# The first sequence of an FFT-mixing and SwiGLU kernel: its unit loop replaced by a written list of steps over eight PSUM banks

## The chip, the cores and the metric

One core of one Trainium2 chip runs one program. The metric is the device time of one execution in microseconds (us). Engine names are those of the profile: PE (TensorE matmul), PEld (TensorE weight load), DVE (VectorE), ACT (ScalarE), POOL (GpSimd), SP (SyncE, which here only issues DMAs).

## The reference

A sequence filter along the time axis, done in frequency space, and a SwiGLU feed-forward layer behind it. Eight sequences of 3008 positions with 256 channels each; the feed-forward layer sees all 24064 positions.

```python
X = np.fft.rfft(x, axis=1)                       # x (8, 3008, 256)
Y = X * (filt_r + 1j * filt_i)[None]
x = np.fft.irfft(Y, n=3008, axis=1).reshape(24064, 256)
xn = x / np.sqrt(np.mean(x * x, -1, keepdims=True) + 1e-06) * rms_g
g = xn @ w_gate                                  # (256, 1536)
out = (g / (1 + np.exp(-g)) * (xn @ w_val)) @ w_out
```

## The kernel before

The transform of length 3008 = 47 x 64 is done as matmuls with tables. Each sequence goes through these units, in this order:

- A: the 64-point step (a0_unit for the first sequence, a_unit for the others), then a change of layout. The first sequence changes layout on the chip: tr0_unit (T), eight groups of PE transposes copied out of PSUM to the tiles t2. The other sequences go through DRAM (z_store, t2_load).
- F: f_unit brings the filter into the layout that the product needs: four PE transposes of 128x128 f32, and two copies to the tile ff. There are twelve: three loads i, filter part f (0 imaginary, 1 real), channel half dh. f_neg (N) makes a negated copy of a piece of ff on POOL, f_last (L) copies one row of it.
- B: b_unit, sixteen units of four matmuls into one PSUM bank: the 47-point step. Unit i is group g = i // 2 of four frequencies and half dh = i % 2.
- P: s_part, two products of the bank with the filter for each unit: e = 0 with the real part, e = 1 with the imaginary part, whose negated copy it also reads. 32 in all. Result in a pair of s tiles.
- Y: yt0_unit, eight matmuls with the identity that add the two products and transpose them, and an eviction to yt.
- I: bi_unit, four matmuls of the inverse 47-point step, and an eviction to uu. After the sixteenth unit, POOL copies a strip of uu to the tile left.

When all of uu is there, t4_first transposes the first four columns on the PE, t4_load transposes all of it by DMA from SP, and first_norm makes the first normalised tile. Then the main loop begins: 8 x 6 x 12 items of the feed-forward layer (gv: gate and value matmuls, Silu on ACT, product on DVE; down: the output matmuls two items later). The mixing work of sequences 1 to 7 is spread over the items of the sequence before by a planner with costs and due times; twelve a_units of sequence 1 fall to the start of the loop, the first two of them before it.

All of it stands in a manual schedule: each engine runs its instructions in the order in which the program issues them. What an instruction waits for comes from its tiles: a tile of a rotating pool of n buffers takes the buffer of the n-th tile before it and waits until that tile's last reader is done, also a reader that stands later in the program.

The POOL queue ahead of the first f_neg is a row of DMA issues: four x_load, six f_load, four loads of tables, then w_load(0) and w_load(1), which load thirds of w_gate and w_val to staging tiles. Staging has four buffers: the three filter tiles, then w_load(0); w_load(1) takes the buffer of filter tile 0. A POOL DMA also waits for the landing of the POOL DMA eight places before it. Behind the loop, w_gain multiplies the staged weights by the norm's gain into wg and wv, two instructions for each third and each of the two weights.

For the first sequence the loop over p (lines 659 to 706) keeps one unit of each kind in flight, with b_unit's bank alternating between two banks:

```python
if 3 <= p < UN:
    b_unit(0, od[p], (0, 3)[p % 2])
    s_part(0, od[p], 1)
...
if 2 <= p < UN + 1:
    yt0_unit(od[p - 2], "A", 1)
...
if 4 <= p < UN + 3:
    bi_unit(0, od[p - 4], "AV"[p == UN + 1], 2)
```

Here "A" is an eviction by ACT, "V" one by DVE. At p == 0 the loop also issues to POOL: the rest of f_neg, w_load(2), wo_load(0) and wo_load(1) (thirds of w_out), x_load(1, 0..2) and the whole of w_gain. After the t4_load transposes, POOL waits for one of them (the copy to seen, line 713) and issues wo_load(2) and x_load(1, 3).

Of the kernel before, what the change touches and what calls it, by code (L numbers as in the profile page):

```python
# [1 line left out]

# [1 line left out]

# [22 lines left out]
K2 = 32  # L27
# [74 lines left out]
def kernel(  # L102
# [31 lines left out]
    xnp = ctx.enter_context(tc.tile_pool(name="xnp", bufs=4))  # L134
    hp = ctx.enter_context(tc.tile_pool(name="hp", bufs=4))
    op = ctx.enter_context(tc.tile_pool(name="op", bufs=2))
    psG = ctx.enter_context(tc.tile_pool(name="psG", bufs=2, space=bass.MemoryType.PSUM))
    psV = ctx.enter_context(tc.tile_pool(name="psV", bufs=2, space=bass.MemoryType.PSUM))
    psO = ctx.enter_context(tc.tile_pool(name="psO", bufs=1, space=bass.MemoryType.PSUM))
    psM = ctx.enter_context(tc.tile_pool(name="psM", bufs=1, space=bass.MemoryType.PSUM))  # L140
    psB = ctx.enter_context(tc.tile_pool(name="psB", bufs=1, space=bass.MemoryType.PSUM))
# [44 lines left out]
            nc.gpsimd.dma_start(t.rearrange("p a d -> p (a d)"), src(N2, XC))  # L186
        st[b]["x"][c] = t

    def bank(i, name):
        pool, tag = ((psM, "mx"), (psG, "pg"), (psV, "pv"), (psB, "mb"), (psO, "po0"))[i]  # L190
        return pool.tile([P, 512], FP32, tag=tag, name=name)

    def copy(eng, out, in_, scale=None):
        if eng == "A":
# [16 lines left out]
        nc.sync.dma_start(dst, st[b]["t1"][c])  # L211

    def t2_tile(b, c):
        if b == 0 and c == 3:
            st[b]["t2"][c] = op.tile([KR, KC, D], FP16, tag="o3", name="t2o")
        else:
            st[b]["t2"][c] = t2p.tile([KR, KC, D], FP16, tag="t2", name="t2")
# [5 lines left out]
    def s_part(b, i, e, eng=None):  # L223
        eng = eng or nc.vector
        g, dh = divmod(i, 2)
        ps, s = st[b]["s"][i]
        fv = ff[:, dh, 4 * g:4 * g + 4, :]
        o = s[e].rearrange("p k (r q) -> p k r q", r=2)
        if e == 0:
            f1 = fv[:, :, 2 * SL:3 * SL].unsqueeze(2).to_broadcast([P, 4, 2, SL])  # L230
            eng.tensor_tensor(out=o, in0=ps, in1=f1, op=ALU.mult)  # L231
        else:
            f2 = fv[:, :, 0:2 * SL].rearrange("p k (r q) -> p k r q", r=2)
            eng.tensor_tensor(out=o, in0=ps[:, :, ::-1, :], in1=f2, op=ALU.mult)  # L234

    def b_unit(b, i, bk=3, e=0):
        g, dh = divmod(i, 2)
        ps = bank(bk, "psb")[:, 0:4 * KR]
        for k in range(4):
            kk = 4 * g + k  # L240
            nc.tensor.matmul(ps[:, ts(k, KR)], st[b]["t2"][kk // KC][:, kk % KC, ds(dh * P, P)],  # L241
                             wb[0:KR, kk, :], start=True, stop=True)
        s = [sp.tile([P, 4, KR], FP16, tag="s%d" % n, name="s%d" % n) for n in range(2)]
        st[b]["s"][i] = (ps.rearrange("p (k r q) -> p k r q", k=4, r=2), s)
        s_part(b, i, e)
# [113 lines left out]
        copy(eng, va[:, dh].rearrange("p k (m i) -> p (k m) i", m=NR)[:, :, 4 * gq:4 * gq + 4],  # L359
             ps.rearrange("p (u t) -> p t u", u=4))  # L360

    def tr0_unit(g, eng):
        pool, tag = ((psO, "po0"), (psO, "po1"), (psM, "mx"))[g % 3]
        ps = pool.tile([KR, 4, 2, P], FP16, tag=tag, name="pst")
        for k in range(4):
            for dh in range(2):
                nc.tensor.transpose(ps[:, k, dh, :], va[:, dh, 4 * g + k, :], ident)  # L367
        c, r = divmod(g, 2)
        if c not in st[0]["t2"]:
            t2_tile(0, c)  # L370
        copy(eng, st[0]["t2"][c][:, 4 * r:4 * r + 4, :].rearrange("p k (e d) -> p k e d", e=2), ps)
# [10 lines left out]
            nc.gpsimd.dma_start(t[:, f].rearrange("p a d -> p (a d)"),  # L382
                                raw(src, row, [[FR4 * D, P], [1, FR4 * D]]))

    def f_unit(i, f, dh, e):
        t = fst[i]
        ps = bank(1 + "AV".index(e), "psf").rearrange("p (a q) -> p a q", a=FR4)
        for a in range(FR4):
            nc.tensor.transpose(ps[:, a, :], t[:, f, a, ds(dh * P, P)], idf)  # L389
        v = ps.rearrange("p a (q s) -> p s a q", s=16)  # L390
        fk = ff[:, dh, 0:K2].rearrange("p (t k) c -> p t k c", k=4)
        fu = ff[:, dh, 1:K2 + 1].rearrange("p (t k) c -> p t k c", k=4)[:, ::-1, ::-1, :]
        lo = SL * (1 + f) + 8 * i
        hi = lo + H
        if i < 2:
            copy(e, fk[:, :, :, lo:lo + 8], v[:, 0:8])
            copy(e, fu[:, :, :, hi:hi + 8], v[:, 8:16])
        else:
            copy(e, fk[:, :, :, lo:lo + 8], v[:, 8:16])
            copy(e, fu[:, :, :, hi:hi + 7], v[:, 0:8, :, 1:8])  # L400
# [6 lines left out]
    def f_neg(k0, n, dhs=(0, 1)):  # L407
        for dh in dhs:
            nc.gpsimd.tensor_scalar(out=ff[:, dh, k0:k0 + n, 0:SL], in0=ff[:, dh, k0:k0 + n, SL:2 * SL],
                                    scalar1=-1.0, scalar2=1.0, op0=ALU.mult, op1=ALU.mult)  # L410
# [122 lines left out]
    def gv(b, m, jt):  # L533
        n = nq(b, m)
        xn = st[b]["xn"][m]
        parts = ((0, 2), (2, 4)) if (b, m, jt) in SPLIT else ((0, n),)
        sg = hp.tile([P, 512], FP16, tag="sg", name="sg")
        hh = hhs[(6 * JT * b + JT * m + jt) % 4]
        made = []
        for q0, q1 in parts:  # L540
            w = (q1 - q0) * P
            pg = psG.tile([P, 512], FP32, tag="pg", name="pg")
            pv = psV.tile([P, 512], FP32, tag="pv", name="pv")
# [53 lines left out]
    def wo_load(q):  # L597
        nc.gpsimd.dma_start(wo[:, ts(q, JT // 3), :],
                            moe_w_out.rearrange("(jt p) d -> p jt d", p=P)[:, ts(q, JT // 3), :])

    def w_gain(q):
        cols = ts(q, DFF // 3)
        t = wst.pop(q)
        for k, dst in enumerate((wg, wv)):
            for dt_ in range(2):
                nc.gpsimd.tensor_scalar(out=dst[:, dt_, cols], in0=t[:, k, dt_, :],
                                        scalar1=gsb[:, dt_:dt_ + 1], scalar2=1.0,
                                        op0=ALU.mult, op1=ALU.mult)

    with tc.manual_schedule():  # L610
        nc.vector.memset(ss3[0], 0.0)
# [44 lines left out]
        a0(3)  # L656
        fill(4)
        a0(4, 5)
        todo = [(i, f, dh) for i in range(2) for f in range(2) for dh in range(2)][:7] + [(2, 0, 0)]
        for u in todo[0:2]:  # L660
            f_unit(*u, "A")
        for g in range(7):
            tr0_unit(g, "V")
            if g < 6:
                f_unit(*todo[g + 2], "A")
        f_neg(4, 4, (0,))
        f_neg(8, 8, (0,))
        UN = K2 // 2
        od = [2, 4, 6, 3, 5, 7, 0, 1] + list(range(8, UN))
        tr0_unit(7, "V")  # L670
        for p in range(2):
            b_unit(0, od[p], (0, 3)[p], 1)
        f_unit(1, 1, 1, "A")
        f_unit(2, 0, 1, "A")
        b_unit(0, od[2], 4, 1)
        f_unit(2, 1, 0, "A")
        for p in range(3):
            s_part(0, od[p], 0)
        for p in range(UN + 3):
            if 3 <= p < UN:  # L680
                b_unit(0, od[p], (0, 3)[p % 2])
                s_part(0, od[p], 1)
            if p == 0:
                f_unit(2, 1, 1, "A")
                f_neg(4, 12, (1,))
                f_last()
                f_neg(0, 4)
                w_load(2)
                wo_load(0)
                f_neg(16, 16)  # L690
                wo_load(1)
                for c in range(3):
                    x_load(1, c)
                for q in range(3):
                    w_gain(q)
            if 2 <= p < UN + 1:
                yt0_unit(od[p - 2], "A", 1)
            if p == UN + 1:
                yt0_unit(UN - 1, "V", 1, slice(0, 2))
                yt0_unit(UN - 1, "A", 0, slice(2, 4))  # L700
            if 4 <= p < UN + 3:
                bi_unit(0, od[p - 4], "AV"[p == UN + 1], 2)
            if UN + 1 <= p < UN + 3:
                fill(1, 1)
# [8 lines left out]
        nc.gpsimd.tensor_copy(out=seen, in_=st[0]["t4"][1][:, 0, 0:4])
        wo_load(2)
        x_load(1, 3)
        first_norm()

        items = [(b, m, jt) for b in range(B) for m in range(6) for jt in range(JT)]
# [166 lines left out]
```

## Time and profile before

| | |
|---|---|
| median of 3 runs | 863.09 us (863.01 to 863.34) |
| the profiled execution's own time | 863.15 us |
| its span, first to last instruction | 861.4 us |
| PE busy in the span | 852.4 us (99%) |
| DVE, ACT, POOL busy | 557.2, 612.4, 297.8 us |
| granted PE clock, mean | 0.999 |
| first F unit on PE | 13.03 us |
| a_unit(1, 0) on PE, behind the last I unit | 38.48 us |
| first gate matmul of the main loop | 43.38 us |

Times inside the span count from its first instruction. The stretch from 13.03 to 43.38 us holds all the work that the diff touches and its tail; from there on the rows follow the planner. A row of the timeline is: start, duration, engine, line, operation, tiles written and read, form, count, and in brackets the engine's idle time before it with what ended it. Start to start of two rows of a busy engine is the price of one instruction there; the duration is a little longer, as the next one starts before the end.

### The profile page before, as it was taken

To read this page: it belongs to the slowest core of one execution; us is meant where nothing else is said; L and a number is where in the kernel's file an instruction comes from. 1 tells how busy PE (TensorE), PEld (TensorE's weight loads), DVE (VectorE), ACT (ScalarE), POOL (GpSimd) and SP (SyncE) were. 2 spreads that over 40 slices of the span, in tenths; PEclk is the share of its full clock that TensorE was granted. 3 is DMA by queue.
4 is the path that set the end of the run, shared out by engine and by line. 5 is a ranking of instruction groups with operands and counts; after the bars stand their busy time and mean duration, and the time that the engine had idled before them with its cause. 6 is when DMAs were issued, how large, how long until landed. Compare 5 with 4: busy or idle time off the path is not lost.

```text
span 861.4 us, 17024 instructions
## 1 busy us (share of the span) xinstructions
PE 852.4 (99%) x6142; PEld 532.2 (62%) x6142; DVE 557.2 (65%) x926; ACT 612.4 (71%) x1339; POOL 297.8 (35%) x346
## 2 busy tenths in 40 slices
PE   8999999999999999999999999999999999999997
PEld 6755666566666666666666666666666666665664
DVE  5857655776666666666666676767666665555554
ACT  4986777787588756887577856888567765777443
POOL 5725742453144322534034430444123430132000
PEclk9999999999999999999999999999999999999999
DMA  9995778765975476656755548433564331521101
GB/s 283 270 204 124 150 164 168 139 130 121 197 137 129 121 150 111 151 107 147 139 127 113 132 98 180 108 87 101 131 127 93 97 70 42 124 54 49 62 25 50
DMA packets 198237, 107.98 MB, mean 125 GB/s; under 512 B 158566, under 2 KB 182520, under 8 KB 198152
## 3 DMA queue, kind: packets, MB, share of 16 engines
q1 hardware_dynamic: 189464, 85.52, 44.1%
q0 software_dynamic: 8544, 21.24, 12.7%
q8 instruction: 48, 0.79, 0.4%
q14 instruction: 37, 0.30, 0.1%
q10 hardware_dynamic: 144, 0.13, 0.0%
HBM read 45.78 MB, written 35.65 MB: 95 GB/s over the span
## 4 chain that ended last, share of the span: by engine, by line
PE 96%; DMA 1%; ACT 1%; DVE 1%; issue 0%; POOL 0%; POOLq 0%
PE po L563 28%; PE pg L546 28%; PE pv L546 28%; PE psb L241 3%; PE psi L285 3%; PE psn L314 2%; PE psa L206 2%; DMA fs<-in_filt_i_dram 1%; PE psy L418 1%; PE psf L389 1%; PE pst L367 0%; ACT sg L550 0%; POOL xc L186 0%; DVE s L231 0%; DVE hh L551 0%
## 5 line engine op out<-in xcount | busy, mean ns | idle before, releaser
L551 DVE TENSOR_TENSOR hh<-pv,sg 128x512 f16<-128x512 f32 (+2 forms) x578 | 391.5, 678 | 286.4 <-ACT sg L550 221.9
L550 ACT ACTIVATE sg<-pg 128x512 f16<-128x512 f32 (+2 forms) x578 | 337.4, 584 | 217.6 <-PE pg L546 213.4
L546 PE MATMUL pg<-xn,wg 128*128 128x512 f16 (+2 forms) x1156 | 338.1, 374 | 0.1
L546 PE MATMUL pv<-xn,wv 128*128 128x512 f16 (+2 forms) x1156 | 338.1, 374 | 0.0
L563 PE MATMUL po<-wo,hh 128*128 128x256 f16 x2256 | 332.7, 273 | 0.0
L563 PEld LDWEIGHTS <-hh 128*128 128x128 f16 x2256 | 213.4, 98 | 105.5 <-issue 0.6
L268 POOL TENSOR_TENSOR ss<-s,s 128x384 f16<-128x384 f16 x112 | 101.9, 911 | 273.2 <-DVE s L234 245.2
L546 PEld LDWEIGHTS <-wv 128*128 128x128 f16 x1156 | 112.9, 98 | 130.7
L546 PEld LDWEIGHTS <-wg 128*128 128x128 f16 x1156 | 111.4, 98 | 17.0 <-issue 0.3
L340 POOL TENSOR_TENSOR xt<-y,rho 128x1024 f16<-128x1024 f32 (+1 forms) x46 | 85.4, 1856 | 2.8
L322 ACT ACTIVATE junk<-y 128x256 f16<-128x256 f32 x180 | 74.3, 413 | 2.8
L231 DVE TENSOR_TENSOR s<-psb,ff 128x384 f16<-128x384 f32 x124 | 67.6, 547 | 0.7 <-ACT ff L195 0.6
L234 DVE TENSOR_TENSOR s<-psb,ff 128x384 f16<-128x384 f32 x124 | 67.6, 546 | 0.0
L195 ACT ACTIVATE uu<-psi 128x384 f16<-128x384 f32 (+1 forms) x127 | 61.6, 486 | 1.5 <-DMA out_dram<-o 0.5
L195 ACT ACTIVATE y<-psn 128x512 f32<-128x512 f32 (+1 forms) x95 | 55.7, 588 | 4.2
L285 PEld LDWEIGHTS <-yt 96*128 96x128 f16 x512 | 35.4, 97 | 26.7 <-issue 1.0
L332 POOL TENSOR_TENSOR rho<-u,mhalf 128x4 f32<-128x4 f32 (+1 forms) x46 | 46.5, 1010 | 3.8
L330 POOL TENSOR_SCALAR u<-ss 128x4 f32<-128x4 f32 (+1 forms) x46 | 8.9, 193 | 104.8 <-ACT junk L322 103.8
L195 ACT ACTIVATE t<-psa 128x512 f16<-128x512 f32 x70 | 41.4, 594 | 3.1 <-PE psa L206 1.7
L285 PE MATMUL psi<-wi,yt 96*128 96x96 f16 x512 | 42.9, 205 | 0.1
L241 PE MATMUL psb<-wb,t 96*128 96x96 f16 x480 | 40.1, 206 | 0.3 <-DVE s L234 0.2
L241 PEld LDWEIGHTS <-t 96*128 96x128 f16 x480 | 28.7, 97 | 12.8 <-DVE s L234 3.3
(101 smaller groups left out, 366.2 us busy)
## 6 DMA issues: line engine op xcount, KB each, us to landing
out_dram<-o SPq DMA_DIRECT2D x40, 512.0 KB, 3.6
xc<-in_x_dram POOLq DMA_DIRECT2D x31, 384.0 KB, 5.6
z_tmp<-t SPq DMA_DIRECT2D x28, 384.0 KB, 2.7
t<-z_tmp SPq DMA_DIRECT2D x28, 384.0 KB, 6.0
out_dram<-o SPq DMA_DIRECT2D x7, 384.0 KB, 2.7
fs<-in_filt_i_dram POOLq DMA_DIRECT2D x3, 512.0 KB, 10.8
fs<-in_filt_r_dram POOLq DMA_DIRECT2D x3, 512.0 KB, 11.2
ws<-in_moe_w_gate_dram POOLq DMA_DIRECT2D x3, 512.0 KB, 9.8
```

Source lines behind the costliest of these rows:

```text
L195: nc.scalar.activation(out=out, in_=in_, func=AXT.Copy, **({} if scale is None else {"scale": scale}))
L231: eng.tensor_tensor(out=o, in0=ps, in1=f1, op=ALU.mult)
L234: eng.tensor_tensor(out=o, in0=ps[:, :, ::-1, :], in1=f2, op=ALU.mult)
L241: nc.tensor.matmul(ps[:, ts(k, KR)], st[b]["t2"][kk // KC][:, kk % KC, ds(dh * P, P)], wb[0:KR, kk, :], start=True, stop=True)
L268: nc.gpsimd.tensor_tensor(out=ss3[g % 3][:, :, dh, 0:KR], in0=s[0], in1=s[1], op=ALU.add)
L285: nc.tensor.matmul(ps[:, k, :], yt[0:KR, k, dh, :], wi[0:KR, 4 * g + k, :], start=True, stop=True)
L322: nc.scalar.activation(out=junk, in_=y[:, i, ts(u, D)], func=AXT.Square, accum_out=ss[:, 2 * i + u:2 * i + u + 1])
L340: nc.gpsimd.tensor_tensor(out=xt[:, 0:n, :], in0=y.rearrange("p a (u d) -> p (a u) d", u=2)[:, 0:n, :], in1=rho[:, 0:n].unsqueeze(2).to_br ...
L546: nc.tensor.matmul(ps[:, 0:w], wt[:, dt_, ts(jt, P)], xn[:, q0:q1, dt_, :], start=(dt_ == 0), stop=(dt_ == 1))
L550: nc.scalar.activation(out=sg[:, c], in_=pg[:, 0:w], func=AXT.Silu)
L551: nc.vector.tensor_tensor(out=hh[:, c], in0=pv[:, 0:w], in1=sg[:, c], op=ALU.mult)
L563: nc.tensor.matmul(po[s4 // 2][:, s4 % 2, :], hh[:, ts(s4, P)], wo[:, jt, :], start=(jt == 0 and s4 % 2 == 0), stop=(jt == JT - 1 and (s4 ...
```

## The change

The loop over p is replaced by a list of 127 steps, walked in order. A step is a letter for the unit, its arguments, its evicting engine (A or V) and, behind a colon, its PSUM bank. The eight banks get names: mx, mb, o0, o1, g0, g1, v0, v1 (the pools psG and psV now have two named tiles of one buffer each, in place of one tile of two buffers; "g" and "v" alone alternate). G is a half of a w_gain third, W, O and X are w_load, wo_load and x_load(1, .), Z is a fill matmul.

Units 8 and 9 carry an "s": b0_unit copies their bank to SBUF by ACT (a tile of the pool xn) and their two products each run on POOL. Two more pairs of s tiles come from the hh tiles of the main loop. Three F units and six T units are evicted by DVE, nine F units and two T units by ACT, and four I units and three halves of Y15 and I15 by DVE. On POOL, f_neg is sixteen instructions of one unit each; wo_load(1), x_load(1, 2), the second half of w_gain(1) and all of w_gain(2) come after the list, and of these wo_load(1), x_load(1, 2) and the last half of w_gain come after the copy to seen.

```diff
-    psG = ctx.enter_context(tc.tile_pool(name="psG", bufs=2, space=bass.MemoryType.PSUM))
-    psV = ctx.enter_context(tc.tile_pool(name="psV", bufs=2, space=bass.MemoryType.PSUM))
+    psG = ctx.enter_context(tc.tile_pool(name="psG", bufs=1, space=bass.MemoryType.PSUM))
+    psV = ctx.enter_context(tc.tile_pool(name="psV", bufs=1, space=bass.MemoryType.PSUM))
...
+    BANKS = {"mx": (psM, "mx"), "mb": (psB, "mb"), "o0": (psO, "po0"), "o1": (psO, "po1"),
+             "g0": (psG, "pg0"), "g1": (psG, "pg1"), "v0": (psV, "pv0"), "v1": (psV, "pv1")}
+    turn = {"g": 0, "v": 0}
...
     def t2_tile(b, c):
-        if b == 0 and c == 3:
+        if b == 0 and len(st[b]["t2"]) == 3:
...
+    def b0_unit(i, bk, soft):
+        g, dh = divmod(i, 2)
+        ps = bank(bk, "psb")[:, 0:4 * KR]
+        for k in range(4):
+            kk = 4 * g + k
+            nc.tensor.matmul(ps[:, ts(k, KR)], st[0]["t2"][kk // KC][:, kk % KC, ds(dh * P, P)],
+                             wb[0:KR, kk, :], start=True, stop=True)
+        if soft:
+            v = xnp.tile([P, 512], FP32, tag="xn", name="v0")[:, 0:4 * KR]
+            copy("A", v, ps)
+            ps = v
+        st[0]["s"][i] = (ps.rearrange("p (k r q) -> p k r q", k=4, r=2), s0_free.pop(0))
...
-    def w_gain(q):
+    def w_gain(q, k):
         cols = ts(q, DFF // 3)
...
-        todo = [(i, f, dh) for i in range(2) for f in range(2) for dh in range(2)][:7] + [(2, 0, 0)]
-        for u in todo[0:2]:
-            f_unit(*u, "A")
-        for g in range(7):
-            tr0_unit(g, "V")
-            if g < 6:
-                f_unit(*todo[g + 2], "A")
...
+        STEPS = """
+            F001A:g0 F000V:g1 T0A:v0 T4V:o1 T6V:v1 T5V:o0 F010A:g1 F100A:v0 T1V:mx T2V:g0 T3V:g1 T7A:v1 F200V:o0
+            F201A:g0 N02 F101V:v0 F110A:v1 B6:mb N03 B4:mx N01 P4.1 F011A:o0 P6.1 B2:o1 P2.1 N11 N06 F210A:v1
+            B3:g1 N16 N13 P3.1 B8s:o0 F111A:g0 F211A:v0 B7:o0 P4.0 N05 N15 P2.0 N04 P6.0 Y4A:mx P7.1 B5:v1 N12
+            Y2A:o1 Y6A:g0 B9s:o1 B10:mx P5.0 P5.1 P8.0 P3.0 L P7.0 N10 P10.1 I4A:mb P8.1 Y5A:v0 I6A:g0 B1:v1
+            Y7A:o1 P10.0 N07 P1.1 W2 Y3A:mb B11:mx N00 B0:g0 I2A:v0 O0 P1.0 P11.0 Y10A:o0 B12:v1 P11.1 P12.1
+            P12.0 I5A:g1 Y8A:mb N17 P0.0 X0 I10A:o0 P0.1 Y1A:v0 P9.0 B13:o1 I3A:mb P13.1 B14:v1 P13.0 Y12A:g1
+            Y11A:mx Y0A:mb P14.1 N14 I7A:o0 P14.0 B15:g0 Y13A:g1 P15.0 P15.1 I12V:v0 X1 G0 G1 G2 Y14A:o1 P9.1
+            I0V:v1 I11V:o0 I8A:mx Y9A:mb I1A:g0 Y15aV:g1 I14A:v0 Y15bV:o1 I13V:mb I9A:v1 I15aV:o0 Z1:mx I15bA:o1"""
+
+        s0_free = [[sp.tile([P, 4, KR], FP16, tag="s%d" % n, name="s%d" % n) for n in range(2)]
+                   for _ in range(4)]
+        s0_free += [[hhs[2 * i + n][:, 0:4 * KR].rearrange("p (k q) -> p k q", k=4) for n in range(2)]
+                    for i in range(2)]
...
+            elif k == "P":
+                u, e = a.split(".")
+                s_part(0, int(u), int(e), nc.gpsimd if u in soft else None)
...
         for c in range(NXC):
             t4_load(0, c)
+        w_gain(1, 1)
+        w_gain(2, 0)
         nc.gpsimd.tensor_copy(out=seen, in_=st[0]["t4"][1][:, 0, 0:4])
+        wo_load(1)
+        x_load(1, 2)
+        x_load(1, 3)
         wo_load(2)
-        x_load(1, 3)
+        w_gain(2, 1)
         first_norm()
```

In the list F201A is filter load 2, part 0, half 1; T4V is group 4; N02 is f_neg of half 0, group 2; P4.1 is unit 4, e = 1; Y15a and Y15b are the two halves of unit 15.

More of the change, by code (lines that the diff above doesn't have):

```diff
@@ L1 @@
 from contextlib import ExitStack
+from functools import partial
 import numpy as np
@@ L187, in x_load, with bank @@
         st[b]["x"][c] = t
-    def bank(i, name):
-        pool, tag = ((psM, "mx"), (psG, "pg"), (psV, "pv"), (psB, "mb"), (psO, "po0"))[i]
-        return pool.tile([P, 512], FP32, tag=tag, name=name)
+    BANKS = {"mx": (psM, "mx"), "mb": (psB, "mb"), "o0": (psO, "po0"), "o1": (psO, "po1"),
+             "g0": (psG, "pg0"), "g1": (psG, "pg1"), "v0": (psV, "pv0"), "v1": (psV, "pv1")}
+    turn = {"g": 0, "v": 0}
+    def bank(i, name, shape=(P, 512), dt=FP32):
+        if not isinstance(i, str):
+            i = ("mx", "g", "v", "mb", "o0")[i]
+        if i in turn:
+            turn[i] += 1
+            i += "01"[turn[i] % 2]
+        pool, tag = BANKS[i]
+        return pool.tile(list(shape), dt, tag=tag, name=name)
     def copy(eng, out, in_, scale=None):
@@ L360, in a0_unit, with tr0_unit @@
              ps.rearrange("p (u t) -> p t u", u=4))
-    def tr0_unit(g, eng):
-        pool, tag = ((psO, "po0"), (psO, "po1"), (psM, "mx"))[g % 3]
-        ps = pool.tile([KR, 4, 2, P], FP16, tag=tag, name="pst")
+    def tr0_unit(g, eng, bk):
+        ps = bank(bk, "pst", (KR, 4, 2, P), FP16)
         for k in range(4):
@@ L383, in f_load, with f_unit @@
                                 raw(src, row, [[FR4 * D, P], [1, FR4 * D]]))
-    def f_unit(i, f, dh, e):
+    def f_unit(i, f, dh, e, bk):
         t = fst[i]
-        ps = bank(1 + "AV".index(e), "psf").rearrange("p (a q) -> p a q", a=FR4)
+        ps = bank(bk, "psf").rearrange("p (a q) -> p a q", a=FR4)
         for a in range(FR4):
@@ L541, in gv @@
             w = (q1 - q0) * P
-            pg = psG.tile([P, 512], FP32, tag="pg", name="pg")
-            pv = psV.tile([P, 512], FP32, tag="pv", name="pv")
+            pg, pv = bank("g", "pg"), bank("v", "pv")
             for ps, wt in ((pg, wg), (pv, wv)):
@@ L599, in wo_load @@
                             moe_w_out.rearrange("(jt p) d -> p jt d", p=P)[:, ts(q, JT // 3), :])
-    def w_gain(q):
+    def w_gain(q, k):
         cols = ts(q, DFF // 3)
[L603 to L608, printed above, removed]
+        for dt_ in range(2):
+            nc.gpsimd.tensor_scalar(out=(wg, wv)[k][:, dt_, cols], in0=wst[q][:, k, dt_, :],
+                                    scalar1=gsb[:, dt_:dt_ + 1], scalar2=1.0, op0=ALU.mult, op1=ALU.mult)
     with tc.manual_schedule():
@@ L658 @@
         a0(4, 5)
-        todo = [(i, f, dh) for i in range(2) for f in range(2) for dh in range(2)][:7] + [(2, 0, 0)]
-        for u in todo[0:2]:
-            f_unit(*u, "A")
-        for g in range(7):
-            tr0_unit(g, "V")
-            if g < 6:
-                f_unit(*todo[g + 2], "A")
[L666 to L685, printed above, removed]
-                f_last()
[L687 to L704, printed above, removed]
@@ L705 @@
-        bi_unit(0, UN - 1, "V", 3, slice(0, 2))
-        bi_unit(0, UN - 1, "A", 0, slice(2, 4))
-        a_unit(1, 0, "A", 1)
+        STEPS = """
[7 more added lines that the diff above has]
+            I0V:v1 I11V:o0 I8A:mx Y9A:mb I1A:g0 Y15aV:g1 I14A:v0 Y15bV:o1 I13V:mb I9A:v1 I15aV:o0 Z1:mx I15bA:o1"""
@@ new lines @@
+        s0_free = [[sp.tile([P, 4, KR], FP16, tag="s%d" % n, name="s%d" % n) for n in range(2)]
+                   for _ in range(4)]
+        s0_free += [[hhs[2 * i + n][:, 0:4 * KR].rearrange("p (k q) -> p k q", k=4) for n in range(2)]
+                    for i in range(2)]
+        halves = {"": slice(0, 4), "a": slice(0, 2), "b": slice(2, 4)}
+        soft = set()
+        for step in STEPS.split():
+            head, _, bk = step.partition(":")
+            k, a = head[0], head[1:]
+            if k == "F":
+                f_unit(int(a[0]), int(a[1]), int(a[2]), a[3], bk)
+            elif k == "T":
+                tr0_unit(int(a[0]), a[1], bk)
+            elif k == "N":
+                f_neg(4 * int(a[1]), 4, (int(a[0]),))
+            elif k == "L":
+                f_last()
+            elif k == "B":
+                if a[-1] == "s":
+                    soft.add(a[:-1])
+                b0_unit(int(a.rstrip("s")), bk, a[-1] == "s")
+            elif k == "P":
+                u, e = a.split(".")
+                s_part(0, int(u), int(e), nc.gpsimd if u in soft else None)
+            elif k == "Y" or k == "I":
+                u = a[:-1].rstrip("ab")
+                (yt0_unit if k == "Y" else partial(bi_unit, 0))(int(u), a[-1], bk, halves[a[len(u):-1]])
+                if k == "Y" and a[len(u):-1] != "a":
+                    s0_free.append(st[0]["s"][int(u)][1])
+            elif k == "Z":
+                fill(int(a), bk)
+            elif k == "W":
+                w_load(int(a))
+            elif k == "O":
+                wo_load(int(a))
+            elif k == "X":
+                x_load(1, int(a))
+            elif k == "G":
+                w_gain(*divmod(int(a), 2))
@@ L708 @@
+        a_unit(1, 0, "A", "g0")
         t4_first()
-        a_unit(1, 1, "V", 0)
-        fill(1, 3)
+        a_unit(1, 1, "V", "mx")
+        fill(1, "mb")
         for c in range(NXC):
             t4_load(0, c)
+        w_gain(1, 1)
+        w_gain(2, 0)
         nc.gpsimd.tensor_copy(out=seen, in_=st[0]["t4"][1][:, 0, 0:4])
+        wo_load(1)
+        x_load(1, 2)
+        x_load(1, 3)
         wo_load(2)
-        x_load(1, 3)
+        w_gain(2, 1)
         first_norm()
```

## The prediction

> **What bounds the kernel now.** First the page, for what the whole program waits for.
>
> ```profile
> PE 852.4 (99%) x6142; PEld 532.2 (62%) x6142; DVE 557.2 (65%) x926; ACT 612.4 (71%) x1339; POOL 297.8 (35%) x346
> ```
>
> The PE is busy for 852.4 of 861.4 us, and from the first gate matmul on it stops for nothing. So the edit can only move the time at which the main loop starts, and add stalls inside the loop. Second, the busy time by stretches (length; PE, PEld, DVE, ACT, POOL busy with counts; PE clock, DMA share, GB/s).
>
> ```profile
> 13.00:21.00 8.00, 7.97 (x108) 7.98 (x109) 5.64 (x9) 5.22 (x17) 4.68 (x8) 1.00 1.04 413
> 21.00:37.00 16.00, 15.03 (x243) 13.22 (x241) 15.31 (x33) 14.59 (x35) 14.12 (x25) 1.00 1.11 316
> 43.40:855.00 811.60, 811.00 (x5651) 500.42 (x5650) 525.15 (x859) 581.18 (x1267) 269.51 (x295) 1.00 0.55 118
> ```
>
> From 21 to 37 us four engines are nearly full at once: PE 15.0, DVE 15.3, ACT 14.6, POOL 14.1 of 16. Work taken from DVE must land where there is room, and POOL has none. Third, the POOL timeline, as POOL is where the change puts it, with the last rows of DVE and two of PE.
>
> ```profile
> 15.35 0.61 PE L389 MATMUL psf<-tab,fs 128*128 128x128 f32 x4
> ...
> 18.59 0.70 POOL L594 DMA_DIRECT2D ws<-in_moe_w_gate_dram  x1 [0.83 <-PE pst L367]
> 19.28 0.72 POOL L594 DMA_DIRECT2D ws<-in_moe_w_val_dram  x1
> 20.28 0.84 POOL L409 TENSOR_SCALAR ff<-ff 128x192 f32<-128x192 f32 x2 [0.27 <-ACT ff L195]
> ...
> 24.04 0.66 POOL L409 TENSOR_SCALAR ff<-ff 128x192 f32<-128x192 f32 x2
> 24.65 0.78 POOL L594 DMA_DIRECT2D ws<-in_moe_w_gate_dram  x1
> 25.43 0.73 POOL L594 DMA_DIRECT2D ws<-in_moe_w_val_dram  x1
> 26.16 0.77 POOL L598 DMA_DIRECT2D wo<-in_moe_w_out_dram  x1
> ...
> 30.95 1.62 POOL L606 TENSOR_SCALAR wg<-ws,gsb 128x512 f16<-128x512 f32 x2
> 32.30 1.57 POOL L606 TENSOR_SCALAR wv<-ws,gsb 128x512 f16<-128x512 f32 x2
> ...
> 36.47 0.54 DVE L234 TENSOR_TENSOR s<-psb,ff 128x384 f16<-128x384 f32 x1
> ...
> 46.02 0.18 POOL L713 COPY seen<-t 128x4 f16<-128x4 f16 x1 [6.64 <-DMA t<-uu]
> ...
> 54.30 0.60 PE L206 MATMUL psa<-xc,tab 128*128 128x512 f16 x2
> ...
> 80.87 1.00 POOL L234 TENSOR_TENSOR s<-y,ff 128x384 f16<-128x384 f32 x1
> ```
>
> w_load(1) (18.59) stands at the head of POOL's queue, and every f_neg and so every e = 1 product is behind it. It waits for two things: the landing of the ninth POOL DMA (issued at 6.30, 11.7 us to landing: 18.0) and the last reader of filter tile 0, which is the fourth F unit of load 0 (at 15.35, so long done). Here the first decides.
>
> **Part 1: the wait of w_load(1).** The list moves that fourth F unit (F011A) behind seven other F units, eight T and two B. In the rows of before a pair of F and T takes 0.89 us on the full PE, so one takes 0.445; a B takes 0.17. F011A is the ninth F: 13.03 + 17 x 0.445 + 0.34 = 20.95, and its end is seen by others 0.17 later (first F pair done on PE 13.03 + 0.45, ACT starts at 13.70): 21.1. The bank of each of these steps is free in time if the evictions take what they take now. A POOL DMA leaves 0.28 us after what it waited for (landing at 6.02, issue at 6.30). So w_load(1) leaves at 21.4, its second half 0.70 later, and N02 starts at 22.9 in place of 20.28: 2.6 us late. Queued behind it on POOL: everything that follows. DVE's first product, P4.1, needs N02, so it starts at 23.3 (21.20 before). DVE has nothing else in its queue meanwhile.
>
> **Part 2: DVE.** Before: 32 products at 0.465 (starts 25.32, 25.79, 26.25), the last ending at 37.0. After: 28 of them = 13.0, so 36.3. Four I units (0.465 each) and three halves (0.3) come on top, 2.8 us, which makes 39.1 with no stall, against 38.96 before. Taking the products of two units off DVE saves 1.9 us and adding evictions gives that back; the late start uses up the rest. F and T on DVE (5.6 us) lie between 13.5 and 20.5, where it idles now.
>
> **Part 3: POOL, which I take to be the new bound.** P9.1, the last soft product, stands behind nearly all of POOL's work, and Y9 on PE needs it. From N02 on, start to start: 16 f_neg pieces at 0.33 = 5.3 (24.04 row); L two copies, 0.4; four products of 128x384 at 0.97 (79.91 to 80.87), 3.9; W2 two DMA issues, 0.78 + 0.73 = 1.5; O0 0.8; X0 and X1 0.55 each, 1.1 (three in 1.65); G0, G1, G2 six instructions at 0.667 (30.95, 32.30, 33.63: two in 1.33) = 4.0. Sum 17.0. The chain has no other wait: the bank copies of units 8 and 9 and the filter tiles are there earlier. P9.1 ends at 22.9 + 17.0 = 39.9. The 16 small pieces of f_neg cost 1.3 us more than the larger pieces of before (768 elements took 0.85, four times 192 take 1.32).
>
> **Part 4: the tail.** Behind Y9 the PE's order has I1, Y15a, I14, Y15b, I13, I9, I15a, Z1, I15b. Y9 to its eviction's start is 0.69 (23.92 to 24.61), then ACT runs Y9 0.49, I1, I14, I9 0.38 each and the half I15b 0.24: 39.95 + 0.69 + 0.49 + 1.14 + 0.24 = 42.5. uu is complete at 39.0 now (ACT's rows end at 39.02). The front is 3.5 us later. t4_first, first_norm and t4_load hang on uu alone, so the first gate matmul goes from 43.38 to 46.9.
>
> **Part 5: loads behind seen.** POOL issues wo_load(1), x_load(1, 2), x_load(1, 3), wo_load(2) behind the copy to seen, in place of wo_load(2), x_load(1, 3). The same transfers, of the same sizes and in the same places, left at 46.15 and 46.94 before, landing 6.0 and 8.2 us later (DMA view: 256 and 384 KB). In times of before, wo_load(1) is there at 52.2 and its first use is the fifth output tile at 53.00: hidden, with 0.8 to spare. x_load(1, 2) is there at 55.1, and a_unit 6 runs at 54.30: the PE, in order, stands still for 0.85. x_load(1, 3) has its use at 57.99 and wo_load(2) at 59.73: hidden, though by one more transfer only. The gain halves are done by 50.3 in the same scale and first used at 56.7.
>
> [...]
>
> **Parts without a row.** T on ACT (128x1024 f16) has no row: at least one 512-wide eviction (0.59) and at most two (1.19); I take 1.0, as 128 elements more cost 0.11 (Y 0.49, I 0.38). Two of them lie beside PE work and no B needs them soon; ACT has 9 F at 0.58, 2 T, 2 copies, 15 Y at 0.49, 11 I at 0.38 and a half I, 19.8 us of work in 28. The two bank copies by ACT are taken as an I (0.38). The eight named banks hold the same memory, and in the main loop g0 and g1 alternate as the two buffers did: nothing. On SP nothing is moved.
>
> **Sum.** Against the profiled execution (863.15, 0.06 above the median): + 3.5 + 0.85 = 867.5. On the low end POOL's pieces at the shortest starts seen (0.31, 0.95) take off 0.4, and no x stall 0.85: 866.2. On the high end pieces under DVE load at 0.5 (the second of the 20.28 pair, with twice the elements) add up to 2: 869.5.
>
> **Rivals.**
>
> *w_load(1) is not held.* For it: its PE wait cost nothing before. Against: the buffer's last reader does move. N02 at 20.28, P9.1 at 37.3, uu at 39.9: + 0.9 + 0.85, 864.9.
>
> *Faster: POOL is not the bound and DVE is.* For it: POOL's spans are rough, and DVE loses 1.9 us. Products from 21.2, 13.0 + 2.8 behind it, uu at 37.0: 2.0 earlier, less the x stall 1.15: 862.0, and 861.1 without it. This needs P9.1 done by 36.4 for break-even and by 34.4 for all of it, so no hold at w_load(1) and POOL's 17.0 at 14.1 or less. Against: POOL's starts are regular, 0.667 six times over.
>
> *The PE clock drops.* Before Y9 the PE has no step left from about 36.6 (Y14 behind P14.0 at 35.5, then I0, I11, I8) until 39.9: an idle gap of 3.3 us, where the longest now is 0.8. The row of before: the last matmul ends at 856.6, the granted clock is 1.00 from 859 to 860 and 0.65 from 860 to 861.4, so a fall to half came about 3.8 us after. A fall would make the tail's matmuls like the first ten fills (4.45 us, 0.22 each when warm): about + 2, 869.5. The decision is whether the gap passes 3.4 to 3.8.
>
> [...]
>
> *x_load(1, 2) lands in time*, as POOL's queue is empty by then: 866.7.
>
> **How the numbers follow.** Forecast 0.54, in time 0.13, clock 0.13, not held 0.08, DVE-bound 0.12. A measurement of this kernel tells 0.2% (1.7 us) from no change. Faster by more takes two thirds of the DVE case, 0.08; half of "not held" and the rest of it fall inside, 0.08; slower 0.84. The range leaves out DVE-bound and the far end of the clock case: 864.4 to 870.5.
>
> **What would show it.** Right: w_load(1) leaves at about 21.4 with a wait for PE, N02 near 22.9, P4.1 near 23.3; POOL has no idle from N02 to P9.1; P9.1 ends near 39.9 and PE's idle ahead of Y9 is 3 us; the first gate matmul is at 46.9; a wait of PE for xc of 0.8 us near a_unit 6. Wrong: P9.1 ends before 37, or DVE's last product of the list rather than POOL's releases the tail, or the loop starts before 43.4.

## The result and the profile after

The changed kernel takes 868.86 us (median of 4 runs, 868.68 to 869.19), the kernel before 863.18 beside it (4 runs, 863.01 to 863.34): a ratio of 1.0066, interval 1.0049 to 1.0084, so it is slower by 0.7%. The profiled execution took 868.68, 5.53 more than the one of before; its span is 866.9. The first gate matmul is at 48.24 (43.38 before), so 4.86 of the 5.53 are there when the main loop starts.

The page's line of engines, for the question whether the PE works more:

```profile
PE 852.4 (98%) x6141; PEld 532.9 (61%) x6141; DVE 558.4 (64%) x930; ACT 611.5 (71%) x1333; POOL 303.2 (35%) x359
```

PE is busy for the same 852.4 us. The 5.5 us that were added are time in which it stands still. The busy time by stretches (PE, PEld, DVE, ACT, POOL with counts, PE clock, DMA share, GB/s) says where:

```profile
13.00:21.00 8.00, 6.89 (x93) 6.77 (x94) 5.99 (x12) 4.52 (x10) 2.54 (x4) 1.00 1.03 411
21.00:37.00 16.00, 13.27 (x201) 12.74 (x200) 12.95 (x29) 11.23 (x29) 14.03 (x30) 0.89 0.76 247
```

From 21 to 37 us POOL alone is as full as before (14.0 of 16); the busy time of PE, DVE and ACT has come down by 1.8, 2.4 and 3.4 us. From 13 to 21 POOL has lost 2.1 us of work: it waits. The timeline of POOL (start, length, line, output and input, count, and in brackets the idle time ahead with what ended it):

```profile
17.31 0.72 POOL L615 DMA_DIRECT2D ws<-in_moe_w_val_dram  x1 [0.54 <-DMA fs<-in_filt_r_dram]
22.70 0.71 POOL L615 DMA_DIRECT2D ws<-in_moe_w_gate_dram  x1 [4.67 <-PE psb L426]
23.40 0.72 POOL L615 DMA_DIRECT2D ws<-in_moe_w_val_dram  x1
24.24 3.50 POOL L418 TENSOR_SCALAR ff<-ff 128x192 f32<-128x192 f32 x11
...
36.20 1.45 POOL L625 TENSOR_SCALAR wg<-ws,gsb 128x512 f16<-128x512 f32 x2
37.55 1.42 POOL L625 TENSOR_SCALAR wv<-ws,gsb 128x512 f16<-128x512 f32 x2
38.88 1.39 POOL L625 TENSOR_SCALAR wg<-ws,gsb 128x512 f16<-128x512 f32 x2
40.20 1.02 POOL L244 TENSOR_TENSOR s<-v,ff 128x384 f16<-128x384 f32 x1
```

w_load(1) stands for 4.67 us at the head of the queue and leaves at 22.70; the first f_neg starts at 24.24, and without a gap from there the last soft product, P9.1, ends at 41.23. The bracket names PE's psb, the B unit that ran last; what the load needs is the filter unit F011A just ahead of it. PE's rows, in order: the four F units from F200 on, F011A, Y4 (the first Y unit), Y9, and a_unit 6 in the loop:

```profile
19.66 1.94 PE L398 MATMUL psf<-tab,fs 128*128 128x128 f32 x16 [0.69 <-DVE t2o L207]
21.77 0.62 PE L398 MATMUL psf<-tab,fs 128*128 128x128 f32 x4
27.11 1.09 PE L440 MATMUL psy<-tab,s 128*96 128x128 f16 x8 [2.57 <-DVE s L241]
41.28 0.59 PE L440 MATMUL psy<-tab,s 128*96 128x128 f16 x7 [1.25 <-POOL s L244]
59.74 0.61 PE L216 MATMUL psa<-xc,tab 128*128 128x512 f16 x2 [0.42 <-DMA xc<-in_x_dram]
```

F011A ends at 22.39, 0.31 ahead of the load's issue. DVE's first product, P4.1, waits for the first f_neg on POOL:

```profile
24.64 1.95 DVE L244 TENSOR_TENSOR s<-psb,ff 128x384 f16<-128x384 f32 x4 [2.69 <-POOL ff L418]
```

Y9 is released by POOL. The chain of waits (start, length, engine, tile, line) ran in the kernel before along PE and, from 35 us, DVE:

```profile
34.63 0.46 PE psy L418 x8
35.09 0.53 DVE s L231
35.62 0.47 DVE s L234
```

In the changed kernel it goes along POOL for 17 us:

```profile
24.24 3.50 POOL ff L418 x11
...
36.26 1.40 POOL wg L625 x2
37.66 1.31 POOL wv L625 x2
38.96 1.31 POOL wg L625 x2
40.27 0.97 POOL s L244
41.28 0.61 PE psy L440 x7
```

Of the part of this chain after 36.26, 4.0 us are w_gain's: work that nobody needs before the loop stands ahead of the product that the loop waits for.

### The profile page after: what moved, and what is told of

It is laid out like the page before. It is cut to its first block, busy times and chain, and to the rows that moved or that the text cites. A ratio compares the mean times of both kernels' runs of the same rounds, so it can differ in the third digit from the quotient of the medians.

```text
span 866.9 us, 17021 instructions
## 1 busy us (share of the span) xinstructions
PE 852.4 (98%) x6141; PEld 532.9 (61%) x6141; DVE 558.4 (64%) x930; ACT 611.5 (71%) x1333; POOL 303.2 (35%) x359
## 3 DMA queue, kind: packets, MB, share of 16 engines
q0 software_dynamic: 8544, 21.24, 12.6%
## 4 chain that ended last, share of the span: by engine, by line
PE 92%; DMA 3%; POOL 2%; ACT 1%; DVE 1%; issue 1%; SPq 0%; POOLq 0%
PE po L584 28%; PE pg L567 27%; PE pv L567 27%; PE psn L324 2%; PE psi L295 2%; PE psb L251 2%; PE psa L216 2%; DMA xc<-in_x_dram 2%; DMA t<-uu 1%; POOL ff L418 1%; PE psf L398 1%; ACT uu L205 0%; POOL xc L187 0%; DVE hh L572 0%; POOL wg L625 0%
## 5 line engine op out<-in xcount | busy, mean ns | idle before, releaser
L244 DVE TENSOR_TENSOR s<-psb,ff 128x384 f16<-128x384 f32 x119 | 64.9, 548 | 2.7 <-POOL ff L418 2.7
L241 DVE TENSOR_TENSOR s<-psb,ff 128x384 f16<-128x384 f32 x119 | 64.9, 547 | 0.3 <-PE psb L426 0.2
L205 ACT ACTIVATE uu<-psi 128x384 f16<-128x384 f32 x124 | 60.2, 488 | 1.1 <-PE psi L295 0.2
L251 PE MATMUL psb<-wb,t 96*128 96x96 f16 x432 | 36.2, 206 | 0.3 <-DVE s L244 0.3
L324 PE MATMUL psn<-t,tab 128*128 128x512 f16 x92 | 34.4, 374 | 0.1
```

The source lines that it names most:

```text
L205: nc.scalar.activation(out=out, in_=in_, func=AXT.Copy, **({} if scale is None else {"scale": scale}))
```

## The experiments

Three things were open: whether the hold of w_load(1) and the order of POOL's queue each carry their share, whether the PE clock had a part in it, and whether the late x_load(1, 2) could be had for nothing. All edits are against the changed kernel, save in e8. "pg0" is the first gate matmul. The kernel before took 863.01, 863.36 and 863.31 in the three groups of runs (e1 to e4; e5 to e8; e9 to e11). Where no interval is given, the time is one run, and the place of pg0 in the trace decides.

**e3, the hold.** F011A goes to right behind F010A, its bank to mb:

```diff
- T5V:o0 F010A:g1 F100A:v0 ... N01 P4.1 F011A:o0 P6.1
+ T5V:o0 F010A:g1 F011A:mb F100A:v0 ... N01 P4.1 P6.1
```

> The changed kernel with the step F011A moved up behind F010A, into bank mb. Theory (w_load(1) holds POOL until the last reader of filter tile 0 is done): w_load(1) leaves at about 20 instead of 22.70, bound by the landing of the ninth POOL DMA; the first f_neg starts at 21.6 instead of 24.24, P9.1 ends 2.6 earlier at 38.6, the first gate matmul at 45.6; no idle of PE over 2 us ahead of Y4 and no drop of its clock. Rival (the landing of the filter loads, 1.5 later than before, sets the start): the first f_neg moves by less than 0.5, the first gate matmul stays near 48.

Measured: 866.82. POOL's timeline:

```profile
18.84 0.70 POOL L615 DMA_DIRECT2D ws<-in_moe_w_gate_dram  x1 [0.82 <-PE pst L376]
20.30 0.72 POOL L615 DMA_DIRECT2D ws<-in_moe_w_val_dram  x1 [0.76 <-DMA wb<-wb_t]
21.14 3.19 POOL L418 TENSOR_SCALAR ff<-ff 128x192 f32<-128x192 f32 x10
...
37.12 1.03 POOL L244 TENSOR_TENSOR s<-v,ff 128x384 f16<-128x384 f32 x1
```

The first f_neg starts 3.10 earlier and P9.1 ends 3.08 earlier, at 38.15: the chain of 17.0 us moves as a whole with w_load(1). The hold is shown (e11, below, has the same edit and ends P9.1 2.77 earlier than the changed kernel). But pg0 came only 1.90 earlier, at 46.34. The windows tell where the rest went:

```profile
35.49:38.90 3.41, 0.95 (x19) 0.81 (x17) 0.80 (x2) 1.16 (x4) 2.66 (x4) 1.00 0.78 145
38.90:42.31 3.41, 3.41 (x34) 2.65 (x32) 1.58 (x4) 2.48 (x6) 0.41 (x2) 0.50 0.03 5
```

The PE now idles 2.46 us ahead of Y9; its clock is halved from 38.90 to 42.31, which is the tail, and the tail (from the end of P9.1 to uu whole) takes 3.69 instead of 2.63.

**e11, the clock in the tail.** e3, with ten filler matmuls, whose result nobody reads, in the gap ahead of Y9:

```diff
- I8A:mx Y9A:mb
+ I8A:mx Z10:mb Y9A:mb
```

> The changed kernel with F011A behind F010A, as in the run before with that edit alone, and ten fill matmuls into the free bank mb ahead of Y9, where PE idled for 2.46 us and its clock then was 0.5 from 38.9 to 42.3. Theory (the tail behind P9.1 took 3.7 us instead of 2.6 because of that clock): P9.1 ends at 38.1 again, the clock stays at 1.00, uu is whole at 40.8 instead of 41.84 and the first gate matmul at 45.2 instead of 46.34. Rival (something else of that order lengthens the tail): the tail stays at 3.7.

Measured: 865.73, and a clock of 1.00 from 8 to 60 us:

```profile
35.20:38.60 3.40, 3.20 (x27) 1.61 (x25) 1.29 (x3) 1.64 (x4) 3.26 (x5) 1.00 0.98 186
```

P9.1 ends 0.31 later than in e3, as the filter load that w_load(1) waits for landed later (19.34, 18.29 in e3); yet pg0 is at 45.48, 0.86 earlier: the tail is back at 2.64. So the clock drop on the tail cost 1.05 us in e3.

**e4, the clock where the changed kernel loses it.** In the changed kernel the clock is halved from 26.63 to 30.04, behind the idle time ahead of Y4. Ten fillers go there:

```diff
- B7:o0 P4.0
+ B7:o0 Z10:v1 P4.0
```

> The changed kernel with ten fill matmuls more, into the free bank v1, behind B7, where PE idles from 24.5 to 27.1 and its granted clock then is 0.5 from 26.6 to 30.0. Theory (POOL's queue): the clock stays at 1.00, DVE's products end about 1 us earlier, at 37.7, and the first gate matmul stays at 48.2 within 0.1, as P9.1 on POOL is where it was. Rival (the clock's drop costs time): the first gate matmul comes 0.7 to 1.4 earlier.

Measured: 870.47. The clock held there and DVE's products ended 1.13 earlier (37.54), but P9.1 ended at 41.05 against 41.23: the cold stretch costs the changed kernel nothing, as POOL sets the end. The time went up since the PE, done with its other work earlier, now idled 2.52 ahead of Y9 and the clock fell on the tail instead (4.0 us; pg0 49.41). The two stretches, before and in the drop:

```profile
37.46:40.87 3.41, 1.13 (x21) 0.93 (x19) 1.61 (x4) 1.97 (x5) 3.41 (x6) 1.00 1.06 200
40.87:44.28 3.41, 3.17 (x34) 3.18 (x35) 1.08 (x3) 1.49 (x4) 0.18 (x1) 0.50 0.10 20
```

**e2, POOL's queue.** w_gain's six instructions go behind P9.1:

```diff
- X1 G0 G1 G2 Y14A:o1 P9.1
+ X1 Y14A:o1 P9.1 G0 G1 G2
```

> The changed kernel with G0, G1, G2 behind P9.1 instead of ahead of it. Theory (POOL's queue releases the tail): P9.1 ends 4.0 us earlier, at 37.2; Y9 then follows I8 on PE at 39.8 instead of 41.28, the first gate matmul comes 1.4 earlier, at 46.8; DVE, whose products end at 38.7, is the next bound, so not all of the 4.0 is seen. Rival (DVE and the cold PE set the front, POOL's wait lies beside them): the first gate matmul stays at 48.2.

Measured: 866.09, pg0 at 45.52. POOL's timeline:

```profile
35.90 1.12 POOL L244 TENSOR_TENSOR s<-v,ff 128x384 f16<-128x384 f32 x1
36.90 1.45 POOL L625 TENSOR_SCALAR wg<-ws,gsb 128x512 f16<-128x512 f32 x2
```

P9.1 ends at 37.02, 4.2 earlier. The loop starts 2.7 earlier, twice what was expected: N02 came 0.3 earlier, and the clock did not drop (1.00 from 8 to 60 us), so that DVE, which is the bound now, ended its products at 37.44 instead of 38.67. A stall of 0.77 ahead of a_unit 6 stayed.

**e6, both.** e3 and e2 together.

> The changed kernel with both: F011A behind F010A, and G0, G1, G2 behind P9.1. Theory: the two terms of POOL's queue are gone, P9.1 ends near 34.2, and DVE's products, which end near 34.7, are the next bound; the tail behind them 3.7, uu whole at 38.4, the first gate matmul at 42.8, 0.6 ahead of the kernel before; the PE's wait for xc at a_unit 6 (0.6 to 0.8) eats that, the span is within 0.4 of the kernel before. Rival (other costs of the list, such as its bank order or ACT's evictions, hold the front): the first gate matmul not before 44.5.

Measured: 863.41, against 863.36 of before. The issue of w_load(1) and P9.1 on POOL:

```profile
19.90 0.70 POOL L615 DMA_DIRECT2D ws<-in_moe_w_gate_dram  x1 [2.14 <-DMA fs<-in_filt_i_dram]
...
33.38 1.11 POOL L244 TENSOR_TENSOR s<-v,ff 128x384 f16<-128x384 f32 x1
```

P9.1 ends at 34.49, DVE's products at 34.97, pg0 is at 43.04, 0.34 ahead of the kernel before; the x stall of 0.59 takes that back. The hold and the order of POOL's queue are together all of what was lost ahead of the loop.

**e5, the soft products back on DVE.**

```diff
- s_part(0, int(u), int(e), nc.gpsimd if u in soft else None)
+ s_part(0, int(u), int(e), None)
```

> The changed kernel with the four soft products of units 8 and 9 on DVE again (the copies of their banks by ACT stay). Theory (POOL's queue releases the tail, and its work is worth less there than the 3.9 us that the four products take): DVE has 32 products from 24.6 on, 14.9 us and 1 us of a cold PE, so its last one ends near 40.5, ahead of POOL's 41.23 in the changed kernel; the first gate matmul at 47.4 to 47.9 instead of 48.24. Rival (DVE is the bound that the soft units relieve): 1.9 us more on DVE, the first gate matmul at 49.5 or later.

Measured: 867.4, pg0 at 47.32. DVE is then the bound: its products end at 40.31, since they start as late as before (N02 24.16). Even so the loop starts 0.9 earlier than with two units on POOL: in this list the two units cost more on POOL, the bound, than they free on DVE.

**e1, the x load.** x_load(1, 2) from behind seen to ahead of w_gain(1, 1):

```diff
+x_load(1, 2)
 w_gain(1, 1)
 w_gain(2, 0)
 nc.gpsimd.tensor_copy(out=seen, in_=st[0]["t4"][1][:, 0, 0:4])
 wo_load(1)
-x_load(1, 2)
 x_load(1, 3)
```

> The changed kernel with x_load(1, 2) moved from behind the copy to seen to right behind the list of steps, ahead of w_gain(1, 1), where POOL is idle. Theory (POOL's queue): the load lands before 50, the wait of PE for xc ahead of a_unit 6 (0.58 us in the changed kernel, 59.16 to 59.74) is gone, the first gate matmul stays at 48.2, the span is 0.6 shorter. Rival (DMA load): the transfer beside the t4_load transposes delays these and the loop's start by as much as it saves, the span stays within 0.2.

Measured: 871.32, 2.6 slower than the changed kernel. The stall ahead of a_unit 6 is gone. But the load leaves at 44.64, beside the t4_load transposes, and their four rows span 11.5 us instead of 8.2, and the copy to seen, which waits for one of them, is at 54.60 instead of 50.89; the rows of SP's queue in the changed kernel and then in e1:

```profile
43.95 8.19 SPq L309 DMA_TRANSPOSE t<-uu  x4
```

```profile
43.80 11.50 SPq L309 DMA_TRANSPOSE t<-uu  x4
```

PE waits for their result, and then for wo_load(1), which POOL issues behind seen, 3.7 later. PE's timeline in e1:

```profile
54.59 0.40 PE L505 MATMUL psn<-tab,t 128*128 128x128 f16 x4 [1.69 <-DMA t<-uu]
...
61.16 0.60 PE L584 MATMUL po<-wo,hh 128*128 128x256 f16 x4 [1.42 <-DMA wo<-in_moe_w_out_dram]
```

The theory that the load could be had for nothing there fell. The rival came true in kind: the transposes were delayed, but the price came inside the loop (pg0 is at 48.09) and was larger than it said.

**e7, three other places at once.** w_load(1) issued behind N12, as its data are needed late; w_gain behind P9.1; all three x loads together, in the place of X0.

```diff
-        w_load(1)
- P7.1 B5:v1 N12 ... N17 P0.0 X0 I10A:o0 ... I12V:v0 X1 G0 G1 G2 Y14A:o1 P9.1
+ P7.1 B5:v1 N12 W1 ... N17 P0.0 X0 X1 X2 I10A:o0 ... I12V:v0 Y14A:o1 P9.1 G0 G1 G2
```

> The changed kernel with w_load(1) issued behind the step N12, so that no f_neg stands behind it; G0, G1, G2 behind P9.1; and x_load(1, 1) and x_load(1, 2) behind x_load(1, 0) in the list, so that x_load(1, 2) is in before the t4_load transposes. Theory: first f_neg at 20 to 21.1, by the landing of the ninth POOL DMA; from there to P9.1 13.0 of the old sum, 1.4 for w_load(1) and 0.55 for the added x_load: P9.1 at 35 to 36.1, uu whole at 37.6 to 38.7, the first gate matmul at 42 to 43.1, no wait of PE for xc at a_unit 6: 0.3 to 1.4 us under the kernel before. Rival (the x loads beside other transfers, or DVE, hold it): first gate matmul after 43.4 or a wait of PE in the loop's first 20 us, not faster than before.

Measured: 863.9 (10 runs, 862.87 to 864.39), ratio to the kernel before 1.0003, interval 0.9993 to 1.0012: no gain, a miss. uu was whole at 38.94, but x_load(1, 0), behind the moved w_load(1) and w_load(2) in the queue and with two more x loads right after it, left at 31.98 and landed at 39.20, and PE's first a_unit of the next sequence waited:

```profile
39.25 0.39 PE L216 MATMUL psa<-xc,tab 128*128 128x512 f16 x1 [0.73 <-DMA xc<-in_x_dram]
```

**e9, the x loads earlier.** e6, with the three x loads ahead of W2 and none behind seen but x_load(1, 3):

```diff
- N07 P1.1 W2 Y3A:mb ... N17 P0.0 X0 I10A:o0
+ N07 P1.1 X0 X1 X2 W2 Y3A:mb ... N17 P0.0 I10A:o0
```

> The changed kernel with F011A behind F010A, G0 to G2 behind P9.1, and x_load(1, 0) to x_load(1, 2) ahead of w_load(2) in the list. Theory: as with the first two alone (first gate matmul 43.04), P9.1 0.5 later by the added x_load and still beside DVE's products, which end near 35; x_load(1, 0) lands near 36, ahead of a_unit(1, 0), and x_load(1, 2) near 41, so neither wait of PE for xc is left: first gate matmul 43.0 to 43.5, the span 0.4 under to 0.2 over the kernel before. Rival (transfers still running at 39 delay t4_load and what hangs on it): a wait of PE in the loop's first 20 us, the span 0.5 or more over.

Measured: 862.87 (10 runs, 862.33 to 863.09), the kernel before 863.31 (19 runs, 863.09 to 863.64); ratio 0.9994, interval 0.9985 to 1.0004. pg0 is at 42.98, 0.40 ahead of before, and no stall follows in the loop. None of its runs is above the lowest of before beside it, but the interval does not exclude 1. It is the best version found, and 6.0 us below the changed kernel. In its POOL timeline the second half of w_load(0) is followed by

```profile
19.83 0.70 POOL L615 DMA_DIRECT2D ws<-in_moe_w_gate_dram  x1 [2.20 <-DMA fs<-in_filt_i_dram]
```

so w_load(1) now waits for the landing of the ninth POOL DMA (the first part of filter load 2, in at 19.27) and no longer for F011A.

**e10, I units on ACT.** e9 with I0 and I11 evicted by ACT, to relieve DVE.

```diff
- I0V:v1 I11V:o0 I8A:mx Y9A:mb
+ I0A:v1 I11A:o0 I8A:mx Y9A:mb
```

> The same with the evictions of I0 and I11 by ACT instead of DVE. Theory (with POOL's terms gone DVE's tail is the bound: 3.7 us behind its last product, 2.8 of it its own evictions): DVE's tail 0.93 shorter, uu whole 0.4 to 0.9 earlier, first gate matmul 42.3 to 42.9, the span 0.4 to 1.0 under the kernel before. Rival (ACT, which gets 0.76 more ahead of Y9, sets the tail): no earlier than without it.

Measured: 863.5 (863.31 to 863.69), ratio 1.0003, interval 0.9994 to 1.0012; pg0 at 43.73. Y9's eviction stands behind three I evictions in ACT's queue, and PE waits for it (0.19 in e9):

```profile
38.07 0.58 PE L295 MATMUL psi<-wi,yt 96*128 96x96 f16 x10 [0.95 <-ACT yt L205]
```

**e8, the hold alone, in the kernel before.** Its list of F units gets the two last readers of filter tiles 0 and 1 exchanged:

```diff
-        todo = [(i, f, dh) for i in range(2) for f in range(2) for dh in range(2)][:7] + [(2, 0, 0)]
+        todo = [(0, 0, 0), (0, 0, 1), (0, 1, 0), (1, 0, 0), (1, 0, 1), (1, 1, 0), (2, 0, 0), (1, 1, 1)]
...
-        f_unit(1, 1, 1, "A")
+        f_unit(0, 1, 1, "A")
```

> The kernel before with the fourth F unit of filter load 0 in the place of the last F unit of load 1, on PE near 20.6 instead of 15.35, and that one in its place. Nothing else is changed. Theory (w_load(1) holds POOL until that unit is done): w_load(1) leaves at 21.4 instead of 18.59, the first f_neg at 22.9 instead of 20.28, DVE's first product near 23.3 instead of 21.20, the first gate matmul 1.0 to 2.0 later than 43.38. Rival (the order of the F units costs nothing by itself, the loss of the change is in its other parts): within 0.3 of 43.38.

Measured: 863.28, pg0 at 43.61, 0.23 later. The expected 1.0 to 2.0 did not come. POOL's row:

```profile
20.04 0.70 POOL L594 DMA_DIRECT2D ws<-in_moe_w_gate_dram  x1 [2.33 <-PE psf L389]
```

The load waited 2.33, though not for F(0,1,1), which is at 20.81 on PE, but for F(1,1,1):

```profile
19.13 0.61 PE L389 MATMUL psf<-tab,fs 128*128 128x128 f32 x4
```

So the load here takes the buffer of tile 1, and not that of tile 0, as the description of the kernel before has it. That fits a load that takes the tile whose last reader stands first in the program; this one run shows it. For the changed kernel, where F011A stands ahead of F111A, both give tile 0. The first f_neg was 1.29 late and DVE's first product 0.78, yet the e = 0 products had to wait for ACT's filter evictions until 23.3 in any case. So the hold that came about was half of the intended one, and its 1.29 us cost 0.23 where POOL is not the bound behind it. What 2.6 us would cost there was not measured.

## Why the prediction was right, and where its sizes were off

The forecast was 867.5 (range 864.4 to 870.5); the profiled execution took 868.68, by the mechanism that the prediction names.

**Part 1, the hold: right in kind, 1.34 us short.** w_load(1) left at 22.70 (21.4 forecast), N02 at 24.24 (22.9), P4.1 at 24.64 (23.3). Two terms were mis-sized, both ahead of F011A. The first F unit started at 13.42 instead of 13.03: 0.29 because the first x load landed later in this execution (the other ten traces with the list lie 0.1 before to 0.27 behind the kernel before), and 0.1 because its bank, g0, was still being emptied by ACT, where the prediction took each bank as free in time. And the F units of filter load 2 were sized by the flow of F and T pairs on the PE, with no term for their data: that load landed at 19.52 (18.03 before), so F200 ran at 19.66, 0.89 beyond the late start. The bracket names DVE there; the landing is 0.14 ahead of the matmul, and in e3, where the load was in at 18.29, F200 ran at 19.23, before that DVE copy ended (19.97). The count of seven F units ahead of F011A should be eight; the sum has eight.

**Part 2, DVE.** The 28 products took 14.0 (13.0 forecast) because the PE fed them at half clock from 26.63 on; e4, with the clock held, brings their end forward by 1.1 (0.2 of it from an earlier start) and P9.1 by 0.2. It was not the bound, as forecast. The aside that DVE idles between 13.5 and 20.5 in the kernel before misreads its own line of 13 to 21 us (5.64 busy of 8.00, with the copies of T); no term of the sum hangs on it.

**Part 3, the POOL chain: exact in sum.** From N02 to the end of P9.1 17.0 forecast, 16.99 measured. The same 17.0 came out in e3, where it started 3.1 earlier. The sum held because POOL's instructions ran back to back, at nearly the lengths that their rows of before had. That it is exact is in part luck: the sixteen f_neg pieces took 0.3 less than forecast (0.31 each, not 0.33), and the DMA issues, the copies of L and the products 0.3 more.

**Part 4, the tail: exact.** 2.6 forecast, 2.63 measured, so that uu was whole at 43.86. The error of part 1 went through undiminished: pg0 at 48.24 instead of 46.9.

**Part 5, the x stall: right in kind, 0.27 too high.** x_load(1, 2) took 7.85 from issue to landing (8.2 in the row of before); a_unit 6 ran 0.58 later than the start of the loop explains. wo_load(1) landed at 56.93, 0.9 before its use: hidden, as forecast.

**Sum.** 867.5 + 1.34 - 0.27 = 868.57; of the last 0.1, 0.06 were added inside the loop, before 122 us. The T evictions by ACT, which had no row, took 1.02 (1.0 taken).

**The rivals.** "Not held" and "DVE is the bound" are refuted by the 4.67 us wait and by the row of Y9, which POOL released; "x_load(1, 2) lands in time" by PE's wait of 0.42 for it. "The clock drops" came true in another place: the gap ahead of Y9 was 1.25 instead of 3.3, because the rest of PE's work was late as well; the drop came behind the gap ahead of Y4, where it cost nothing. That it cost nothing was luck, as the sum had no term for it: in e4, where the clock held ahead of Y4, it fell on the tail. e3 and e4 show the predicted case, with its price at 1.05 to 1.4 rather than 2, after gaps of 2.46 and 2.52 us and not of 3.4 to 3.8.

## What to carry to other kernels

Before work is moved to an engine, read that engine's queue from its first late instruction to the one that others wait for, and add up what stands between: the sum of row lengths came out within 0.1 us here. Then look at both ends of that queue. One filter unit (four transposes) placed late kept a DMA issue, and with it 17 us of work, waiting for a buffer; and six multiplications that nobody needed yet stood ahead of the last product. Two reorderings of the list (e6) gave 5.3 of the 5.5 us back without any change in the work.

## What was not expected of the hardware

**The PE clock fell after idle gaps of 2.46 to 2.57 us in three traces, and held after one of 2.57 us in e2.** In the changed kernel the granted clock is 1.00 from 6.15 to 26.63 us, 0.50 from 26.63 to 30.04 (3.41 us) and 1.00 from there to the end of the loop; the gap ahead of Y4 is 2.57 us. In e3 the clock was 0.50 from 38.90 to 42.31 after a gap of 2.46 us, in e4 from 40.87 to 44.28 after one of 2.52. In the 3.41 us ahead of these drops the PE was busy for 28% (e3, above), 33% (e4, above) and 39% (changed kernel); in e1 the mean clock was 0.56 from 26.40 to 29.80, behind 3.40 us with 1.41 busy. Windows of the changed kernel:

```profile
23.21:26.63 3.42, 1.33 (x16) 1.17 (x15) 1.99 (x5) 1.95 (x7) 3.30 (x10) 1.00 1.03 387
26.63:30.04 3.41, 2.93 (x28) 2.94 (x29) 3.25 (x8) 1.19 (x2) 3.32 (x9) 0.50 0.40 148
```

In e2 the gap ahead of the same Y unit is 2.57 us as well, from 24.24 to 26.81. The two windows that share it have the PE busy for 68% and 50%, and the clock stayed at 1.00 in both and in the next:

```profile
21.90:25.32 3.42, 2.34 (x30) 2.11 (x28) 0.98 (x3) 2.82 (x10) 2.80 (x7) 1.00 1.02 392
25.32:28.73 3.41, 1.72 (x28) 1.60 (x29) 3.41 (x9) 1.20 (x3) 3.41 (x10) 1.00 0.77 287
```

So a gap of 2.57 us came with a drop in one trace and without one in another. With ten fills in the gap the clock held in e4 (ahead of Y4) and in e11 (ahead of Y9). What sets e2 apart from the changed kernel is not shown.

**A packet of the instruction queue went beside a late load.** While the filter load that F200 needs was landing, a 16 KB packet of the queue that the DMA view calls instruction was moved. The view of 17.2 to 18.3 us (queue: packets, MB, share), for the changed kernel:

```profile
q0 software_dynamic: 122, 0.43, 98.3%
q8 instruction: 1, 0.02, 5.8%
```

In the kernel before that queue has no row in this stretch; its packet starts at 18.36. In the changed kernel it starts at 17.30 and takes 1.03 us; fifteen of the load's sixteen landing events are in by 18.30, the last is at 19.52. In the kernel before all sixteen of this load are in by 18.03, and the first load with one so late is the one issued at 10.07: fifteen by 20.04, the last at 21.24. Whether the packet held the late part up, and why it comes earlier with the list, is not shown: no kernel was built to move it alone.

**In e1 a POOL load ran beside the DMA transposes, and these took 3.3 us longer** (11.50 instead of 8.19, with a load of 384 KB). Only one such overlap was made, in one run, so how it depends on the sizes is open.
